# A re-ordered start, a shared last block and re-ordered routing steps in an attention kernel that feeds a mixture of experts

## The chip, the cores and the metric

The kernel runs on one core of one Trainium2 chip. The metric is the time of one execution on the device in microseconds (us); a run's profile gives in addition the span from the first to the last instruction of the core, which is 1 to 2 us shorter (261.74 and 260.6 in the profiled run before). Executions of one kernel are sorted into normal ("fast") and slow ones: of the kernel before, 257.84 to 261.46 us in five, and 262.16 and 262.80 in two. All comparisons here use fast runs, with a 95% interval.

The engines are named as in the profile: PE is TensorE (its weight loads are PEld), DVE is VectorE, ACT is ScalarE, POOL is GpSimd and SP is SyncE.

## The reference

Linear attention over 8 batches of 8 heads, 576 tokens and 64 numbers per head. Its output, 4608 tokens of 512 numbers, goes through the one best of 8 experts for each token.

```python
q_s = softmax(q, axis=-1);  k_s = softmax(k, axis=2)       # over numbers; over tokens
kv  = einsum('bhsd,bhse->bhde', k_s, v)
x   = einsum('bhsd,bhde->bhse', q_s, kv)                    # -> (4608, 512)

logits = x @ w_gate + modality_bias[modality_id]            # (4608, 8)
e_idx, gate_w = argmax(logits), softmax(logits) at e_idx
for e in range(8):
    mask = e_idx == e
    h = maximum(x[mask] @ w1[e], 0.0)                       # 512 -> 1024
    out[mask] = gate_w[mask, None] * (h @ w2[e])            # 1024 -> 512
```

The bias of a modality is large against the logits, so nearly every token goes to one of two experts, one for each modality. The kernel loads the weights of these two alone, computes all tokens with them, and checks by counts at the end whether that was everything (a loop behind it would do the rest; it runs zero times on these inputs).

## The kernel before

For each batch, `attend` makes kv, the logits and their inputs; `route` decides the side (expert) of each token and sorts. Sorting is a matmul with a permutation: side "a" is packed from the left of the array `xs`, side "b" from its right. `slots` and `places` find out which token sits at which place, for the stores. The feed-forward work on `xs` is a generator of *steps*: 8 first-layer matmuls (`h_ps`) or 4 second-layer ones (`y_ps`). `weave` lets a share of these steps run between the parts of a batch, so that PE has work while DVE and ACT go through the routing chain.

```python
CAP = 2432; NSLOT = 2 * CAP                     # places of a side: 19 blocks of 128
FULL = [256 * (b + 1) for b in range(B - 1)] + [CAP]
...
def route(b):
    ...                                         # logits -> kk (expert key) -> isa (side)
    yield 2
    r_ps = ...; matmul(r_ps[:, 0], tri, isa); matmul(r_ps[:, 1], ones, isa)     # places within the batch
    ...                                         # gsum, qi
    tensor_tensor_scan(out=aoff...); tensor_copy(out=aoff_i...)
    scale(0)                                    # x_sb of tile 0 <- x_ps * qi
    tensor_scalar(out=na, in0=isa...); tensor_tensor(out=pos, in0=na, in1=cpos...)
    tensor_tensor(out=pos, in0=pos, in1=r_ps[:, 0, :]...)
    tensor_tensor(out=perm...)
    yield 4
    for t in range(NT):                         # xT_ps = x_sb x perm; ACT copies it to xs at a run-time offset
        ...
def slots(b):                                   # DVE: vals, slot, hi, lo, hhi; POOL: hv = hhi * vals; DVE: hlo
def places(b):                                  # PE: id_ps = hlo x hv; DVE: lst, idb, ab, sel
    ...
    nc.vector.scalar_tensor_tensor(out=idb, in0=lst[:, 0, :], scalar=float(P), in1=lst[:, 1, :], ...)
    nc.vector.tensor_tensor(out=ab, in0=lst[:, 2, :], in1=krow, op=ALU.is_equal)
    nc.vector.scalar_tensor_tensor(out=sel, in0=idb, scalar=-OOB, in1=ab, ...)
...
def mains(n):
    for _ in range(n):
        if now[0] < 16 * len(sorted_) - 4: next(main, None); now[0] += 1
...                                             # the start, in part
alone(r0); slots(0); cast_weights(0, 3, nc.gpsimd); mains(1)
for _ in a1: mains(1)
places(0)
...
for b in range(2, B):
    weave(batch(b), 16 / 28.3, prep(b + 1, nc.gpsimd) if b + 1 < B else (), 4)
```

`prep(b, eng)` casts v of a batch on the named engine and takes the exponentials of k and q on ACT. `cast_weights(side, part, eng)` casts a quarter of an expert's weights to bf16.

The softmax here doesn't subtract the row's maximum and nothing guards it: scores larger than these inputs give would overflow.

Of the kernel before, what the change touches and what calls it, by code (L numbers as in the profile page):

```python
# [42 lines left out]
def kernel(  # L43
# [67 lines left out]
    def load_batch(b, names="kvq", eng=nc.sync):  # L111
        for nm in names:
            src = {"k": k, "v": v, "q": q}[nm]

            t = stage.tile([P, HG, NJ * Dh], FP32, name="st", tag="st")
            eng.dma_start(
                out=t,
                in_=bass.AP(
                    tensor=src.tensor,
                    offset=src.offset + b * H * S * Dh,  # L120
                    ap=[[NJ * Dh, P], [2 * S * Dh, HG], [1, NJ * Dh]],
                ),
            )
            st[nm, b] = t

    load_batch(0)
# [24 lines left out]
    load_batch(1)  # L151
# [67 lines left out]
    nc.gpsimd.memset(lst, 0.0)  # L219
    aoff_i = persist.tile([1, B * NT], I32)  # L220
# [8 lines left out]
    bsel = const.tile([P, B * NT, E], FP32)  # L229

# [42 lines left out]
    def gate_weights():  # L273
        nc.vector.tensor_copy(
            out=view(wgb, [[2 * Dh, E], [1, 2 * Dh]], 0, (0, NP)),
            in_=view(wg_f, [[1, E], [E, 2 * Dh]], 0, (0, NP)),
        )
        w_ps = sp_ps.tile([P, E, NP], BF16, name="w_ps", tag="sp")
        for e in range(E):
            nc.tensor.transpose(out=w_ps[:, e, :], in_=wgb[0:NP, 2 * Dh * e : 2 * Dh * (e + 1)], identity=ident[0:NP, 0:NP])  # L280
        nc.vector.tensor_copy(out=wg_sb, in_=view(w_ps, [[1, NP], [NP, E]]))

    def biases():

        nc.vector.tensor_copy(out=mbf, in_=view(mraw, [[2, NJ], [2 * NJ, 64]]))
        m_ps = sp_ps.tile([P, NT, B], BF16, name="m_ps", tag="sp")
        for t in range(NT):
            j0, nj = (2 * (t - 1), 2) if t else (NJ - 1, 1)
            nc.tensor.transpose(
                out=m_ps[0 : tsz[t], t, :], in_=view(mbf, [[1, 64 * nj]], 64 * j0), identity=ident[0:B, 0:B]  # L290
            )
        modf = const.tile([P, B, NT], FP32, name="modf")
        nc.vector.memset(modf, 0.0)
        nc.vector.tensor_copy(out=view(modf, [[1, NT - 1], [NT, B]], 1), in_=m_ps[:, 1:NT, :])
        nc.vector.tensor_copy(out=modf[0:64, :, 0], in_=m_ps[0:64, 0, :])
        biasd = const.tile([P, E], FP32, name="biasd")
        nc.vector.tensor_sub(out=biasd, in0=bias_b[:, 1, :], in1=bias_b[:, 0, :])
        nc.vector.tensor_tensor(
            out=bsel, in0=view(modf, [[1, B * NT], [0, E]]), in1=view(biasd, [[0, B * NT], [1, E]]), op=ALU.mult
        )  # L300
        nc.vector.tensor_tensor(
            out=bsel, in0=bsel, in1=view(bias_b, [[0, B * NT], [1, E]]), op=ALU.add
        )
# [42 lines left out]
    eks, eqs, last_v, xs_w = {}, {}, [None], []  # L346

    def prep(b, v_eng):
        eks[b] = sb.tile([P, NJ, HG * Dh], BF16, name="ek")
        eqs[b] = sb.tile([P, NJ, HG * Dh], BF16, name="eq")  # L350
        for nm in "kvq":
            src = st.pop((nm, b))
            for g in range(2):
                if nm == "v":
                    last_v[0] = copy_on(
                        v_eng,
                        view(vb_b[b % 2], [[Dh, 2], [260, NJ], [1, Dh]], 130 * g),
                        view(src, [[NJ * Dh, 2], [Dh, NJ], [1, Dh]], 2 * g * NJ * Dh),
                    )
                else:  # L360
                    nc.scalar.activation(  # L361
                        out=view((eks if nm == "k" else eqs)[b], [[Dh, 2], [HG * Dh, NJ], [1, Dh]], 2 * g * Dh),
                        in_=src[:, 2 * g : 2 * g + 2, :],
                        func=ACT.Exp,
                    )
                yield

    def attend(b):
# [38 lines left out]
        for c0, nj in ((0, 4), (4, 4), (8, 1)):  # L407
            tp = tps.tile([P, 1024], BF16, name="tp_ps", tag=tag)
            for jj in range(nj):
                for hp in range(2):  # L410
                    nc.tensor.transpose(  # L411
                        out=view(tp, [[2 * nj * 64, 2], [1, 64]], hp * nj * 64 + jj * 64),
                        in_=eq[:, c0 + jj, P * hp : P * hp + P],
                        identity=ident,
                    )
# [3 lines left out]
                view(tp, [[nj * 64, NP], [1, 64 * nj]]),  # L419
            )  # L420
            if nj > 1:
                yield 1.2 if c0 == 0 else 1.5
        kvT_ps = ka.tile([P, 1024], BF16, name="kvT_ps", tag="ka")
        for p_ in range(NP):
            nc.tensor.transpose(out=kvT_ps[:, P * p_ : P * p_ + P], in_=kvbd[:, p_, :], identity=ident)
        kvT = small.tile([P, NP * P], BF16, name="kvT")
        nc.scalar.copy(out=kvT, in_=kvT_ps[:, 0 : NP * P])
# [71 lines left out]
    def route(b):  # L499
# [19 lines left out]
        )  # L519
        xps = [x_tile(b, 0)]  # L520
        yield 1.6
        xps.append(x_tile(b, 1))
        yield 2
# [8 lines left out]

        nc.vector.tensor_tensor_scan(
            out=aoff[:, o + 1 : o + 1 + NT],
            data0=ones[:, 0:NT],
            data1=r_ps[:, 1, :],
            initial=aoff[:, o : o + 1],
            op0=ALU.mult,
            op1=ALU.add,
        )  # L540
        nc.vector.tensor_copy(out=aoff_i[:, o : o + NT], in_=aoff[0:1, o : o + NT])
# [12 lines left out]
        scale(0)  # L554
        na = small.tile([P, NT], FP32, name="na")
        nc.vector.tensor_scalar(out=na, in0=isa, scalar1=0.0, scalar2=None, op0=ALU.is_equal)
        pos = small.tile([P, NT], FP32, name="pos")
        nc.vector.tensor_tensor(out=pos, in0=na, in1=cpos, op=ALU.mult)
# [12 lines left out]
        yield 4  # L571
        scale(1)
        free[0] = nc.vector
        for t in range(NT):
# [13 lines left out]
            for side, off in (("a", 0), ("b", right)):  # L588
                a = nc.s_assert_within(at[t], 0, b * S + cum[t] - T, skip_runtime_bounds_check_because=WHY)
                w = nc.scalar.copy(out=window(a + off, b, T, off > 0), in_=xT_ps[:, :, 0:T])  # L590
                if b == 0 and t == 0:
                    after(w, xs_w, "every place holds a number, also one that no token comes to")
            yield 1.3 if t < NT - 1 else 2.5
# [59 lines left out]

    def todo_of(ph):
# [12 lines left out]
    def ffn1(lo, w, slot, hT):  # L667

        nf = 512 // w
        for f0 in range(0, KF, nf):  # L670
            h_ps = ff.tile([P, 512], FP32, name="h_ps", tag="ff")
            for f in range(nf):
                for kd in range(KD):
                    nc.tensor.matmul(  # L674
                        out=h_ps[:, f * w : (f + 1) * w],
                        lhsT=W[:, slot, kd * F + (f0 + f) * P : kd * F + (f0 + f + 1) * P],
                        rhs=xs[:, kd, lo : lo + w],
# [10 lines left out]
    def ffn2(w, slot, hT, ix, stores):  # L688
        for t in range(w // P):
            y_ps = ff.tile([P, D], FP32, name="y_ps", tag="ff")  # L690
            for kf in range(KF):
# [3 lines left out]
                    rhs=W[:, slot, W2 + kf * D : W2 + (kf + 1) * D],  # L695
# [3 lines left out]
                if kf == 3:  # L699
                    yield  # L700
            y_sb = ybuf.tile([P, D], FP32, name="y_sb")
# [16 lines left out]
    def second(lo, w, slot, hT):  # L718
        yield from ffn2(w, slot, hT, rows_of(sel, lo, w), "stores")

    def main_pieces():

        late = []
        for ph in range(NPH):
            for slot, lo, w in todo_of(ph):
                hT = hbuf.tile([P, KF, GW], BF16, name="hT")
                yield from ffn1(lo, w, slot, hT)
                late.append((lo, w, slot, hT))
                if len(late) > 1 or (ph, slot) == (0, 0):
                    yield from second(*late.pop(0))  # L730
        yield from second(*late.pop(0))

    main = main_pieces()
    now = [0]

    def mains(n):

        for _ in range(n):
            if now[0] < 16 * len(sorted_) - 4:
                next(main, None)  # L740
# [31 lines left out]
    for b in range(2, B):  # L772
        load_batch(b)
    gate_weights()
    biases()
    token_ids()
    p0, p1 = prep(0, nc.vector), prep(1, nc.gpsimd)
    a0, a1, r0, r1 = attend(0), attend(1), route(0), route(1)
    alone(p0)
    for kd in range(KD):  # L780
        for half in range(2):
            w = nc.gpsimd.memset(view(xs.bitcast(FP32), [[1, NSLOT // 4]], (2 * kd + half) * NSLOT // 4), 0.0)
            after(w, last_v, "GpSimd and VectorE share a port")
            xs_w.append(w)
    for _ in range(7):
        next(a0)
    next(p1)
    next(p1)
    alone(a0)
    next(r0)  # L790
    next(r0)
    next(r0)
    alone(p1)
    cast_weights(0, 0, nc.scalar)
    for _ in range(3):
        next(a1)

    next(r0)
    cast_weights(0, 2, nc.gpsimd)
    next(r0)  # L800
    next(a1)
    next(r0)
    next(a1)
    next(r0)
    next(a1)
    cast_weights(0, 1, nc.vector)
    alone(r0)
    slots(0)
    cast_weights(0, 3, nc.gpsimd)
    mains(1)  # L810
    for _ in a1:
        mains(1)
    places(0)
    cast_weights(1, 0, nc.scalar)
    next(r1)
    mains(1)
    cast_weights(1, 1, nc.scalar)
    next(r1)
    mains(1)
    next(r1)  # L820
    cast_weights(1, 2, nc.scalar)
    cast_weights(1, 3, nc.scalar)
    weave(r1, 0.6)
    slots(1)
    mains(8 - now[0])
# [17 lines left out]
    for b in range(2, B):  # L843
        weave(batch(b), 16 / 28.3, prep(b + 1, nc.gpsimd) if b + 1 < B else (), 4)
# [33 lines left out]
    for _ in main:  # L878
        pass
# [4 lines left out]
    with tc.For_i(0, nr) as e:  # L884
# [28 lines left out]
        for _, _, lo, w in passes:  # L913
            hT = hbuf.tile([P, KF, GW], BF16, name="hT")
            alone(ffn1(lo, w, 0, hT))
            alone(ffn2(w, 0, hT, rows_of(sel1, lo, w), "stores again"))
# [30 lines left out]
```

## Time and profile before

| | before |
|---|---|
| time, median of 3 runs | 261.74 us (258.37 to 262.39) |
| profiled span, mean granted PE clock | 260.6 us, 0.965 |
| PE / DVE / ACT / POOL busy | 202.9 / 148.8 / 144.5 / 81.4 us |
| first kv matmul of batches 2, 3, 7 | 67.66, 89.30, 184.82 us |
| end of the last matmul | 247.8 us |

A line of the timeline gives the start in us, the busy time of the group in us, the engine, the source line, the operation, output and inputs, shapes, the count and, in brackets, how long the engine had been idle before it and what ended that. Three timeline lines of the kernel before are needed later for comparison. The first two are the index arithmetic beside a cast of v on POOL; the third is the choice of side in batch 3, ahead of the sorting.

```profile
121.56 2.24 POOL L343 CAST vb<-st 128x1152 bf16<-128x1152 f32 x2
122.68 1.17 DVE L645 TENSOR_TENSOR ab<-lst,krow 128x38 f32<-128x38 f32 x1
...
128.72 0.23 DVE L517 SCALAR_TENSOR_TENSOR isa<-kk,key,valid 128x5 bf16<-128x5 f32 x1
```

`ab` takes 1.17 us beside POOL's second cast; it takes 0.19 at 47.90, with POOL idle. From `isa` at 128.72 to the first transposed tile at 132.02 (in the prediction) pass 3.30 us. The row of the page that gives PE's granted clock in tenths, in 40 slices of the span:

```profile
PEclk9999999979999869999999999999999999999985
```

The clock is full but for two short stretches, one before batch 2 (0.7 of full speed in the ninth slice, 52 to 59 us) and one at its end (0.8 and 0.6 in the 14th and 15th, 85 to 98 us); the last two slices (0.8 and 0.5) reach past PE's last matmul, which ends at 247.8 us.

### The profile page before, as it was taken

The numbers are of one execution on the slowest core, as the hardware profiler recorded it, in microseconds if no ns is written. First come the engines' busy times: TensorE is split into PE (matmuls) and PEld (weight loads), VectorE is DVE, ScalarE is ACT, GpSimd is POOL, SyncE is SP. The second block draws the span as 40 slices with busy tenths as digits, with TensorE's granted clock in tenths as the row PEclk, the third lists the DMA queues.
The fourth block names the chain that finished last, engine by engine and source line by source line (L and its number), as shares of the span: only waits on it lengthen the run. The fifth ranks groups of instructions, "written<-read, shape, count | busy, mean of one in ns | idle before, by whom it ended". The sixth has DMA issues, their size and how long they took to land. (4 is left out here: it accounts for less than half of the span.)

```text
span 260.6 us, 5319 instructions
## 1 busy us (share of the span) xinstructions
PE 202.9 (78%) x1994; PEld 140.6 (54%) x1994; DVE 148.8 (57%) x506; ACT 144.5 (55%) x230; POOL 81.4 (31%) x95
## 2 busy tenths in 40 slices
PE   0173659569997599898989889898987989999900
PEld 0062547347664475657557565755755656666500
DVE  5476773856628365768776786878658553111210
ACT  1344574797985646668576766756543734442200
POOL 5069205013360234126113611621232133222320
PEclk9999999979999869999999999999999999999985
DMA  6999999998799606932972020111202022221200
GB/s 226 373 391 406 390 400 344 314 381 333 242 378 397 237 3 219 309 139 57 376 227 95 3 81 29 54 43 40 84 3 81 1 83 81 81 83 72 82 16 1
DMA packets 18972, 46.58 MB, mean 179 GB/s; under 512 B 1261, under 2 KB 1261, under 8 KB 18942
## 3 DMA queue, kind: packets, MB, share of 16 engines
q1 hardware_dynamic: 15872, 36.70, 39.3%
q0 software_dynamic: 3040, 9.44, 9.5%
q8 instruction: 17, 0.28, 0.4%
q14 instruction: 13, 0.11, 0.1%
q10 hardware_dynamic: 30, 0.05, 0.1%
HBM read 36.75 MB, written 9.96 MB: 179 GB/s over the span
## 5 line engine op out<-in xcount | busy, mean ns | idle before, releaser
L674 PE MATMUL h_ps<-xs,W 128*128 128x256 bf16 (+1 forms) x640 | 78.9, 274 | 1.5 <-ACT xs L590 1.2
L703 POOL DMA_INDIRECT out_dram<-y_sb,ix x38 | 37.6, 988 | 124.1 <-DVE y_sb L343 48.7
L692 PE MATMUL y_ps<-W,hT 128*128 128x512 bf16 x304 | 74.3, 382 | 0.0
L674 PEld LDWEIGHTS <-W 128*128 128x128 bf16 x640 | 59.1, 100 | 11.3 <-issue 2.6
L685 ACT ACTIVATE hT<-h_ps 128x512 bf16<-128x512 f32 x69 | 40.6, 597 | 35.3 <-PE h_ps L674 32.8
L590 ACT CAST xs<-xT_ps 128x512 f32 (+2 forms) x80 | 38.1, 562 | 10.0 <-PE xT_ps L578 10.0
L692 PEld LDWEIGHTS <-hT 128*128 128x128 bf16 x304 | 27.4, 98 | 25.8 <-issue 0.6
L343 DVE COPY y_sb<-y_ps 128x512 f32<-128x512 f32 x19 | 13.1, 691 | 42.0 <-PE y_ps L692 41.0
L547 DVE TENSOR_TENSOR x_sb<-x_ps,qi 128x512 bf16<-128x512 f32 (+1 forms) x40 | 27.1, 682 | 0.9 <-PE x_ps L470 0.4
L578 PE MATMUL xT_ps<-perm,x_sb 128*128 128x128 bf16 (+1 forms) x160 | 16.0, 226 | 12.5 <-DVE perm L561 9.5
L343 ACT COPY y_sb<-y_ps 128x512 f32<-128x512 f32 x19 | 11.1, 582 | 22.9 <-PE y_ps L692 21.6
L578 PEld LDWEIGHTS <-x_sb 128*128 128x128 bf16 (+1 forms) x160 | 11.4, 103 | 21.0 <-issue 9.1
L361 ACT ACTIVATE eq<-st 128x1152 bf16<-128x1152 f32 x16 | 18.3, 1156 | 7.0 <-DMA st<-in_q_dram 4.7
L620 POOL TENSOR_TENSOR hv<-hhi,vals 128x570 bf16<-128x570 bf16 x8 | 12.5, 1568 | 28.1 <-DVE hhi L616 27.9
L361 ACT ACTIVATE ek<-st 128x1152 bf16<-128x1152 f32 x16 | 18.4, 1166 | 2.0 <-DMA st<-in_k_dram 2.0
L411 PE MATMUL tp_ps<-ident,eq 128*128 128x128 bf16 x144 | 14.1, 247 | 4.2 <-ACT et L343 2.0
L470 PE MATMUL x_ps<-kvbd,et 128*128 128x128 bf16 (+1 forms) x160 | 17.1, 235 | 0.0
L378 PE MATMUL kv_ps<-vb,ek 64*128 64x129 bf16 x288 | 12.8, 251 | 3.9 <-ACT eq L361 2.6
L343 POOL CAST vb<-st 128x1152 bf16<-128x1152 f32 x14 | 15.7, 1145 | 0.0
L411 PEld LDWEIGHTS <-eq 128*128 128x128 bf16 x144 | 11.7, 112 | 7.1 <-issue 3.6
L378 PEld LDWEIGHTS <-ek 64*128 64x128 bf16 x288 | 10.7, 111 | 6.4 <-ACT eq L361 2.7
L470 PEld LDWEIGHTS <-et 128*128 128x128 bf16 (+1 forms) x160 | 11.4, 107 | 4.5 <-issue 2.5
(139 smaller groups left out, 196.9 us busy)
## 6 DMA issues: line engine op xcount, KB each, us to landing
st<-in_k_dram SPq DMA_DIRECT2D x8, 1152.0 KB, 5.7
st<-in_v_dram SPq DMA_DIRECT2D x8, 1152.0 KB, 8.0
st<-in_q_dram SPq DMA_DIRECT2D x8, 1152.0 KB, 9.7
st<-in_moe_w_dram SPq DMA_DIRECT2D x8, 1024.0 KB, 8.7
out_dram<-y_sb,ix POOLq DMA_INDIRECT x38, 2.8
W<-in_moe_modality_id_dram ACTq DMA_DIRECT2D x1, 36.0 KB
hT<-in_moe_w_gate_dram ACTq DMA_DIRECT2D x2, 8.0 KB
bias<-n_moe_modality_bias_dram ACTq DMA_DIRECT2D x1, 0.1 KB
```

Source lines behind the costliest of these rows:

```text
L343: return (nc.scalar.copy if eng is nc.scalar else eng.tensor_copy)(out=out, in_=in_)
L361: nc.scalar.activation(out=view((eks if nm == "k" else eqs)[b], [[Dh, 2], [HG * Dh, NJ], [1, Dh]], 2 * g * Dh), in_=src[:, 2 * g : 2 * g + ...
L378: nc.tensor.matmul(out=kv[hg][:, 130 * hp : 130 * hp + 129], lhsT=ek[rows, j, P * hp : P * hp + P], rhs=vb[rows, j, hp, 0:129], start=(j = ...
L411: nc.tensor.transpose(out=view(tp, [[2 * nj * 64, 2], [1, 64]], hp * nj * 64 + jj * 64), in_=eq[:, c0 + jj, P * hp : P * hp + P], identity ...
L470: nc.tensor.matmul(out=view(x_ps, [[2 * Dh, 2], [1, Dh]], (4 * (p_ % 2) + p_ // 2) * Dh, (0, T)), lhsT=et[:, p_, tcol[t] : tcol[t] + T], r ...
L547: nc.vector.tensor_tensor(out=view(x_out[t], [[2 * Dh, HG], [Dh, 2], [1, Dh]], 0, (0, T)), in0=view(xps[t], [[2 * Dh, HG], [Dh, 2], [1, Dh ...
L578: nc.tensor.matmul(out=xT_ps[:, kd, 0:T], lhsT=x_out[t][0:T, kd * P : (kd + 1) * P], rhs=perm[0:T, t, 0:T], start=True, stop=True,)
L590: w = nc.scalar.copy(out=window(a + off, b, T, off > 0), in_=xT_ps[:, :, 0:T])
L674: nc.tensor.matmul(out=h_ps[:, f * w : (f + 1) * w], lhsT=W[:, slot, kd * F + (f0 + f) * P : kd * F + (f0 + f + 1) * P], rhs=xs[:, kd, lo ...
L685: nc.scalar.activation(out=h_out, in_=h_in, func=ACT.Relu)
L692: nc.tensor.matmul(out=y_ps, lhsT=hT[:, kf, t * P : (t + 1) * P], rhs=W[:, slot, W2 + kf * D : W2 + (kf + 1) * D], start=(kf == 0), stop=( ...
L703: store = nc.gpsimd.indirect_dma_start(out=out, out_offset=bass.IndirectOffsetOnAxis(ap=ix[:, t : t + 1], axis=0), in_=y_sb, in_offset=Non ...
```

## The change

The intent has four parts. One 128-place pass is dropped: the last block of both sides is replaced by one block, whose tokens and weights are copied at a run-time offset for whichever side is larger. The start is re-ordered so that batch 0 is sorted sooner, with v and q of batch 0 (and q of batch 1) loaded in halves. `xs` is cleared in parts, batch by batch. In the routing, the product for the permutation goes ahead of the counts and the scaling of tile 0 behind the permutation. The limit on feed-forward steps becomes a list of which batch each needs. The diff, cut to its core:

```diff
+    def clear(b):                                   # two memsets on GpSimd, left and right
+        lo, hi = S * b, min(S * (b + 1), NSLOT // 2)
+        xs_w[b] = [nc.gpsimd.memset(xs[:, :, c : c + hi - lo].bitcast(FP32), 0.0) for c in (lo, NSLOT - hi)]
+    clear(0)
+    clear(1)
 ...
 def route(b):
+        nc.vector.tensor_scalar(out=na, in0=isa, ...)         # before the counts
+        nc.vector.tensor_tensor(out=pos, in0=na, in1=cpos, ...)
-        yield 2
+        yield 2.4
 ...
-        scale(0)
-        ... na, pos
         ... perm
-        yield 4
+        scale(0)
+        yield 5
 ...
-            if now[0] < 16 * len(sorted_) - 4:
+            if now[0] < len(due) and due[now[0]] < len(sorted_):
 ...                                                 # order of passes from phase 2 on (1, 2: layer; x, y: passes)
+                order += [(ph, 1, x), (ph, 1, y), (ph, 2, x), (ph, 2, y)]
 ...                                                 # the start, from batch 0's sorting on
+    cast_weights(0, 1, nc.scalar)
+    alone(a1)
+    mains(1)
+    r1 = route(1)
+    cast_weights(0, 2, nc.scalar)
+    steps(r1, 1)
+    mains(1)
+    cast_weights(0, 3, nc.scalar)
+    steps(r1, 1)
+    mains(2)
+    steps(r1, 1)
     slots(0)
-    cast_weights(0, 3, nc.gpsimd)
-    mains(1)
-    for _ in a1:
-        mains(1)
+    cast_weights(1, 0, nc.gpsimd)
+    for b in range(2, 5):
+        clear(b)
+    mains(1)
     places(0)
-    cast_weights(1, 0, nc.scalar)
-    next(r1) ...
+    mains(1)
+    weave([next(r1)], 0.6)
+    cast_weights(1, 1, nc.vector)
+    weave(r1, 0.6)
     cast_weights(1, 2, nc.scalar)
     cast_weights(1, 3, nc.scalar)
-    weave(r1, 0.6)
+    mains(12 - now[0])
     slots(1)
 ...
-        weave(batch(b), 16 / 28.3, prep(b + 1, nc.gpsimd) ...)
+        weave(batch(b), (14 if b == 2 else 15.5) / 28.6, prep(b + 1, nc.gpsimd) ...)
 ...                                                 # the tail: which side is larger -> big_w, big_x
+    tail["x"] = ...; nc.vector.tensor_copy(out=tail["x"], in_=<xs at big_x>)
+    for i in range(2):
+        for half in range(2):
+            nc.vector.tensor_copy(out=t[:, ...], in_=<W at big_w + ...>)     # 4 copies of 128x2048 bf16
```

## The prediction

> **What bounds the kernel now.** I read the busy time by stretch first, then the instructions in order of time at each boundary that it shows, then the waits of TensorE (PE). The chain of waits is useless here: it holds two pieces in the last microsecond. The stretches (start:end, length, then busy us of PE, weight load, DVE, ACT, POOL, then the clock, the DMA share and GB/s):
>
> ```profile
> 0.00:37.90 37.90, 15.62 (x192) 13.26 (x193) 24.96 (x92) 17.21 (x22) 16.28 (x36) 1.00 0.98 364
> 37.90:67.60 29.70, 23.29 (x198) 16.66 (x195) 17.68 (x57) 22.46 (x32) 9.38 (x7) 0.94 0.90 319
> 67.60:90.20 22.60, 17.55 (x191) 11.27 (x190) 12.51 (x42) 16.88 (x27) 6.27 (x6) 0.97 0.95 357
> 90.20:115.20 25.00, 23.18 (x223) 16.14 (x223) 15.66 (x53) 15.28 (x27) 6.20 (x6) 0.89 0.48 164
> 212.70:247.80 35.10, 35.09 (x260) 22.39 (x258) 6.61 (x36) 13.08 (x22) 10.45 (x11) 1.00 0.20 74
> ```
>
> Time outside PE work is at the start. Until 37.9 us PE is idle 22.3 us; to 67.6 it is idle another 6.4; to 90.2 another 5.0. Then come batches of 23.07 us (the first kv matmuls of consecutive batches stand at 115.62, 138.69, 161.76 and 184.82), with about 21.3 us of PE work each. The last 35 us are feed-forward work alone, without a hole, so each matmul taken out there is time taken off the end. After PE's last matmul at 247.8 the kernel needs 12.8 us more to its end at 260.6, which the change leaves alone.
>
> Three places matter. First, the first feed-forward matmul:
>
> ```profile
> 13.90 1.42 DVE L343 CAST vb<-st 128x1152 bf16<-128x1152 f32 x2
> 14.80 2.13 PE L378 MATMUL kv_ps<-vb,ek 64*128 64x129 bf16 x36 [2.63 <-ACT eq L361]
> 23.82 2.24 POOL L343 CAST vb<-st 128x1152 bf16<-128x1152 f32 x2
> 23.87 1.15 DVE L505 TENSOR_TENSOR lg<-lg,bsel 128x40 f32<-128x40 f32 x1
> 31.07 1.88 ACT L343 CAST W<-st 128x2048 bf16<-128x2048 f32 x1
> 38.77 1.10 ACT L590 CAST xs<-xT_ps 128x512 f32 x2
> 39.43 1.86 PE L674 MATMUL h_ps<-xs,W 128*128 128x256 bf16 x8 [1.18 <-ACT xs L590]
> ```
>
> It starts at 39.43, released by the ACT copies of sorted tokens, not by the weights: the landing records put the second weight piece at about 27.2 us. The delay accumulates earlier. The v casts of batch 0 stand at 13.90 behind DVE work on gate weights and biases, though v landed at about 10.6; the routing's addition of 40 columns takes 1.15 us beside POOL's v cast; a weight cast of 1.88 us on ACT stands ahead of the copies of sorted tokens.
>
> Second, the end of batch 2:
>
> ```profile
> 88.32 0.38 PE L578 MATMUL xT_ps<-perm,x_sb 128*128 128x128 bf16 x4 [0.63 <-ACT xs L590]
> 89.30 0.29 PE L378 MATMUL kv_ps<-vb,ek 64*128 64x129 bf16 x1 [0.60 <-ACT xs L590]
> 90.27 2.11 PE L378 MATMUL kv_ps<-vb,ek 64*128 64x129 bf16 x35 [0.69 <-ACT xs L590]
> 115.62 1.20 PE L378 MATMUL kv_ps<-vb,ek 64*128 64x129 bf16 x36
> ```
>
> No feed-forward matmul stands between 84.3+1.03 and 92.31. The source says why: with two batches sorted the main work may go to 16x2-4 = 28 steps, and it has run out. PE then waits at every ACT copy, and 35 kv matmuls take 2.11 us where 36 take 1.20 a batch later: the slow clock.
>
> Third, one hole in each batch, and the last blocks:
>
> ```profile
> 132.02 0.27 PE L578 MATMUL xT_ps<-perm,x_sb 64*128 64x64 bf16 x4 [0.80 <-DVE perm L561]
> 237.15 1.95 PE L674 MATMUL h_ps<-xs,W 128*128 128x128 bf16 x32
> 238.93 3.62 PE L692 MATMUL y_ps<-W,hT 128*128 128x512 bf16 x16
> ```
>
> [...]the addition of 1.15 us took 0.20 at 49.00, with POOL idle.[...]
>
> **The change part by part.**
>
> (a) One block less. Both sides carry 19 blocks of 128 places, 38 in all; now the last block of each is dropped and one, chosen at run time, serves whichever side is larger. It saves one 128-wide pass: 32 first-layer matmuls, 1.95 us, and 8 second-layer ones, half of 3.62, 1.81 us. This lies in the full tail: **-3.8 us**. It adds four weight copies (4 x 0.69), a copy of tokens (some 0.4) and a register load on DVE (the like of it, 0.5 us): about 3.7 us. DVE is busy 6.6 of 35.1 us there, and the copies are issued some 25 us ahead of their use. A late output copy may hold a PSUM buffer: I allow +0.4.
>
> (b) The start. I carried the new order through, engine by engine, with durations from the trace. DVE can cast v at 9 to 11.3, so kv ends near 12.5 instead of 16.9. q in halves lets its first exponential go near 12.1, but the second half still lands at 13.6, so the exponentials end at 14.8 instead of 15.8. Logits come near 17.7 (before: 21.9). Routing takes about 3.4 us from there to the choice of side, near 21.2 (before: 26.95), now without POOL's v cast. Then gains shrink: ACT, not POOL, casts v of batch 1 (2.3), and q of batch 1 lands at 22.7, so ACT is held to 25.3. The 10 token copies (10 x 0.56 less the two short ones, 5.2 us) interleave with batch 1's copies (1.6), and DVE does batch 1's kv scaling and the token ids in between; they end near 35. The cast of the second weight piece (1.9) comes after them on ACT: first feed-forward matmul near 37 instead of 39.4. **-2.3 us**, and batch 1's attention is almost done by then (before, its logits came at 44.9).
>
> (c) No starvation. The new order lets 12 steps go with one batch sorted and 32 with two (before 28). 18 are meant to be done before batch 2 starts and 14 over it. So batch 3 starts with 32 steps done rather than 28, the 4 extra ones filling holes: 11.4 us of idle PE lie in 37.9 to 90.2. A step is 8 first-layer or 4 second-layer matmuls, 1.03 us at most and 0.9 pipelined: **-3.7 us**. The slow clock from 88.7 to 95.5 goes too: kv 0.9, two groups of 8 first-layer matmuls 0.85 and 0.4 (1.89 and 1.43 against 1.04), one of transposes 0.45: **-2.6 us**. Since ACT may not fill so neatly, I take 1.2 off these gains.
>
> (d) Batches 3 to 7. The product for the permutation is made before the counts are known, the scaling of the first tile goes behind the permutation, and the wait weighs 5 instead of 4, so 0.45 step more work is in between. The first transposed matmul then needs the scaled tile as well, so of the 0.8 hole I count 0.5 gone: 5 x 0.5 = **-2.5 us**. Main work per batch falls from 16 to 15.5 steps, but what is not done there goes to the tail, no gain.
>
> (e) Memsets of sorted x: eight of 1.11 us at 15.4 to 23.9 become smaller ones, the first four at 5 to 9 us on an idle POOL. No own gain.
>
> Sum: -3.8 +0.4 -2.3 -3.7 -2.6 +1.2 -2.5 = -13.3, from 261.7 to **248.4 us**.
>
> **Rivals.** ACT becomes the bound of the start: it is busy 22.5 of 29.7 us in 37.9 to 67.6 already and gets v of batch 1 and two weight casts beside the relus. For it: each relu there stands behind a 1.9 us cast, and PE waits for it. Against: POOL and DVE keep three casts, as before. Then (b) and half of (c) go: about 253. Second, loading is the bound: it moves 364 GB/s to 37.9 us, so halves of a transfer bring no byte earlier. Against: weights land 12 us before use. Were it so, only (a) and (d) stay: 255 to 256. Third, the end: weight copies that wait (register load, a buffer, an in-order DVE with output copies behind) would stall the tail by some us, giving back (a): 252. Fourth, the batch becomes bound by its own latency once it carries less main work; for it speaks the 1.75 us idle per batch, against it that holes follow single waits; it would cancel (d): 251.
>
> **Range and chances.** Each rival alone leaves a gain of over 2% (below 256.5); two at once are needed to lose it. The three runs before spread from 258.4 to 262.4, so I give 242.5 to 254.5. Faster by over 2%: 0.92, within: 0.07, slower: 0.01.
>
> **What will show it.** (a) 37 stores instead of 38, 608 first-layer matmuls instead of 640 and 296 instead of 304 second-layer ones, and a tail without a hole ahead of the last pass. (b) First h_ps matmul near 37, r_ps of batch 0 near 21.5. (c) No stretch at half clock after 60 us, and feed-forward matmuls between all transposed tiles of batch 2. (d) The hole before the first transposed matmul under 0.4 us, its releaser x_sb, batches of about 22.1 us. I would be wrong if the first h_ps came after 39, if holes moved to another wait (relu behind casts), or if a batch took 23 us with 15.5 steps.

## The result, and the profile after

The changed kernel takes **267.37 us** (median of 4 runs, 267.25 to 268.03) against 260.88 us (258.37 to 262.39) for the kernel before: ratio **1.029** (1.020 to 1.037). It is slower, where the prediction said 5% faster. A ratio here is the mean time of one kernel's fast runs over that of the other's in the same rounds, so it is not quite the ratio of the medians quoted. The profiled spans are 260.6 us before and 265.6 after; the mean clock of these two runs is 0.965 and 0.910.

First, where the span went. Starts of the first kv matmul of a batch cut it into stretches; all numbers are us, read from PE's timeline.

| stretch | before | after | after less before |
|---|---|---|---|
| start to batch 2 | 67.66 | 75.61 | +7.95 |
| batch 2 | 21.64 | 20.49 | -1.15 |
| batch 3 | 26.32 | 23.78 | -2.54 |
| batches 4 to 6 | 69.20 | 71.09 | +1.89 |
| batch 7 to the last matmul | 63.0 | 61.5 | -1.5 |
| after the last matmul | 12.8 | 13.1 | +0.3 |
| span | 260.6 | 265.6 | +5.0 |

The loss is before batch 2. The first two stretches also hold more work than before: by the counts of weight loads, 18 feed-forward steps stand before batch 2 and 13 over it, against 16 and 12. And starts differ between runs: batch 2 starts at 67.66 us in the kernel before and at 64.81 in the experiment with the tail alone (below), whose code is the same up to there. So some 3 us of a difference in this start can be chance; the loss is larger than that.

In the clock row of the changed kernel half clock and mixtures with it (0.5 to 0.9 of full speed; 0.65 on average from 20 to 73 us) reach from the fourth slice to the eleventh, some 20 to 73 us. This is not what makes it slow: other runs of the same kernel with a mean clock of 0.942 and 0.944 took 268.03 and 267.40 us.

```profile
PEclk9995557759799999999999999999999999999975
```

The start itself goes as planned. These are the counts of batch 0 and the first first-layer matmuls behind the weight cast, from the timeline of the changed kernel:

```profile
22.00 0.17 PE L568 MATMUL r_ps<-isa,tri 128*128 128x5 bf16 x1 [2.98 <-DVE isa L556]
...
38.12 1.46 PE L726 MATMUL h_ps<-xs,W 128*128 128x256 bf16 x6 [1.70 <-ACT W L358]
```

`r_ps` stands at 22.00 (27.09 before). Two first-layer matmuls go at 35.84 and the others wait for the second weight piece until 38.12 (39.43 before). The loss comes after that. The timeline of the changed kernel from 49 to 75 us:

```profile
49.80 0.52 PE L676 MATMUL id_ps<-hv,hlo 64*128 64x114 bf16 x5 [4.10 <-POOL hv L659]
...
51.52 4.56 POOL L228 MEMSET xs<- 128x1152 f32 x6
...
52.01 4.09 DVE L690 TENSOR_SCALAR ix<-sel 128x2 int32<-128x2 f32 x1
...
52.09 4.02 DVE L580 TENSOR_TENSOR x_sb<-x_ps,qi 128x512 bf16<-128x512 f32 x1
...
56.19 0.61 PE L617 MATMUL xT_ps<-perm,x_sb 128*128 128x128 bf16 x4 [3.52 <-DVE x_sb L580]
...
63.03 3.71 ACT L358 CAST W<-st 128x2048 bf16<-128x2048 f32 x2
...
67.29 6.19 PE L726 MATMUL h_ps<-xs,W 128*128 128x256 bf16 x40 [2.69 <-ACT hT L737]
...
74.87 0.17 DVE L690 TENSOR_SCALAR ix<-sel 128x2 int32<-128x2 f32 x1
```

There are three holes on PE, 10.3 us together:

1. **4.10 us** for `id_ps`. `slots(0)` now stands directly ahead of `places(0)`, and in DVE's list, which the trace shows worked off in order, it stands behind batch 1's permutation (45.38) and first scaling (46.12): its first instruction starts at 46.73. POOL's product `hv` ends only at 49.75, and on PE nothing behind `id_ps` starts in that time. Before, feed-forward steps and batch 1's attention lay between the two.
2. **3.52 us** for a transposed tile. Six memsets of `xs`, a row of 4.56 us on POOL, hold a DVE instruction of two numbers per partition (`ix`) for 4.09 us; the same instruction takes 0.17 at 74.87. The held one ends at 56.10, the row of memsets at 56.08. The scaling of the next tile (`x_sb`) is queued behind it: it is recorded from 52.09 and ends at 56.11. Not every instruction is held: at the start of the same trace, in the row of the first four memsets (4.88 to 9.02 us), casts of 16 and of 2 numbers (`parts`) take 1.26 and 0.90 us (0.15 for 16 numbers at 4.31, ahead of the row), and a subtraction of two SBUF inputs between them, at 5.99, takes 0.16.
3. **2.69 us** for first-layer matmuls: the relu that frees their buffer waits behind two weight casts, 3.71 us, on ACT.

Second, the batches. The timeline of the changed kernel around the index arithmetic in batch 4:

```profile
128.08 2.56 DVE L681 SCALAR_TENSOR_TENSOR idb<-lst 128x38 f32<-128x38 f32 x1
...
128.35 2.24 POOL L358 CAST vb<-st 128x1152 bf16<-128x1152 f32 x2
...
131.35 0.67 PE L479 MATMUL lg_ps<-gx,et 128*128 128x18 bf16 x20 [0.89 <-DVE gx L474]
```

Here an instruction of two SBUF inputs (`idb`) is held over both casts of v, 2.56 us, where before `ab` was held over one, 1.17 us; the logits behind it now wait 0.89 us. (`ab` is recorded from 122.68, 1.12 us into two casts of 2.24. `idb` is recorded from 128.08 and the casts from 128.35, so which of them came first the trace does not settle.) This stands in batches 3 and 4 alone; in batches 5 and 6 `idb` takes 0.20 us. And a batch carries less main work than the prediction's 15.5 steps: between 120.6 and 145.0 us 64 weight loads of the first layer stand as before, but 28 of the second layer instead of 32, that is 8 + 7 = 15 steps instead of 16. (`weave` starts its account at zero in each batch, so 15.5 is cut to 15. Of the 14 meant for batch 2, 13 are done.) The window's answer for the second layer, with start:end, length, and busy us of PE and of the weight loads:

```profile
120.60:145.00 24.40, 6.54 (x25) 2.48 (x28) 1.00 0.54 187
```

(25 matmuls are recorded for 28 loads: some matmul records are missing, so the loads are counted.)

The tail goes as planned. Timeline of the changed kernel:

```profile
224.97 2.50 DVE L996 COPY st<-W 128x2048 bf16 x4
...
245.35 1.95 PE L726 MATMUL h_ps<-x_sb,st 128*128 128x128 bf16 x32
...
250.59 1.89 PE L744 MATMUL y_ps<-st,hT 128*128 128x512 bf16 x8
```

The weight copies are done 18 us ahead of their use (227.5 and 245.35 us), 37 stores, 608 first-layer matmuls and 296 weight loads of the second layer are recorded, and no hole stands before the last pass.

### The profile page after: what moved, and what is told of

The parts are those of the page before. It is cut to its first block, busy times and chain, and to the rows that moved or that the text cites.

```text
span 265.6 us, 5231 instructions
## 1 busy us (share of the span) xinstructions
PE 200.6 (76%) x1934; PEld 137.4 (52%) x1954; DVE 151.4 (57%) x501; ACT 153.8 (58%) x241; POOL 78.7 (30%) x94
## 5 line engine op out<-in xcount | busy, mean ns | idle before, releaser
L726 PE MATMUL h_ps<-xs,W 128*128 128x256 bf16 x576 | 74.2, 282 | 4.7 <-ACT hT L737 2.7
L744 PE MATMUL y_ps<-W,hT 128*128 128x512 bf16 x268 | 68.9, 386 | 1.3 <-issue 0.3
L757 POOL DMA_INDIRECT out_dram<-y_sb,ix x37 | 36.7, 991 | 111.9 <-DVE y_sb L358 29.9
L726 PEld LDWEIGHTS <-W 128*128 128x128 bf16 x576 | 55.7, 101 | 14.3 <-issue 3.6
L737 ACT ACTIVATE hT<-h_ps 128x512 bf16<-128x512 f32 x73 | 42.0, 596 | 21.1 <-PE h_ps L726 20.3
L629 ACT CAST xs<-xT_ps 128x512 f32 (+2 forms) x80 | 38.8, 563 | 13.6 <-PE xT_ps L617 13.3
L358 ACT COPY y_sb<-y_ps 128x512 f32<-128x512 f32 x22 | 12.9, 586 | 43.2 <-PE y_ps L744 40.9
L580 DVE TENSOR_TENSOR x_sb<-x_ps,qi 128x512 bf16<-128x512 f32 (+1 forms) x40 | 29.8, 764 | 1.2 <-PE x_ps L509 0.5
L358 DVE COPY y_sb<-y_ps 128x512 f32<-128x512 f32 x15 | 10.4, 692 | 33.0 <-PE y_ps L744 33.0
L393 PE MATMUL kv_ps<-vb,ek 64*128 64x129 bf16 x288 | 12.8, 239 | 5.9 <-DVE vb L358 2.8
L393 PEld LDWEIGHTS <-ek 64*128 64x128 bf16 x288 | 10.3, 104 | 9.7 <-issue 7.6
L358 POOL CAST vb<-st 128x1152 bf16<-128x1152 f32 x12 | 13.5, 1152 | 0.0
```

The source lines that it names most:

```text
L358: return (nc.scalar.copy if eng is nc.scalar else eng.tensor_copy)(out=out, in_=in_)
L393: nc.tensor.matmul(out=kv[hg][:, 130 * hp : 130 * hp + 129], lhsT=ek[rows, j, P * hp : P * hp + P], rhs=vb[rows, j, hp, 0:129], start=(j = ...
L580: nc.vector.tensor_tensor(out=view(x_out[t], [[2 * Dh, HG], [Dh, 2], [1, Dh]], 0, (0, T)), in0=view(xps[t], [[2 * Dh, HG], [Dh, 2], [1, Dh ...
L629: w = nc.scalar.copy(out=window(a + off, b, T, off > 0), in_=xT_ps[:, :, 0:T])
L726: nc.tensor.matmul(out=h_ps[:, f * w : (f + 1) * w], lhsT=w1(kd * F + (f0 + f) * P, P), rhs=x_in[:, kd, :], start=(kd == 0), stop=(kd == K ...
L737: nc.scalar.activation(out=h_out, in_=h_in, func=ACT.Relu)
```

## The experiments

Sixteen kernels ran, in four calls; all gave the correct result. The kernels of a call share the runs of the kernel before on the same chip; its medians, over all its runs, slow ones among them, were 259.85, 261.92, 261.48 and 259.23 us in that order.

### First call: each hole by itself

**Clears earlier.** If the row of memsets makes hole 2, moving it away should give that hole back.

```diff
     cast_weights(0, 0, nc.gpsimd)
+    for b in range(2, 5):
+        clear(b)
 ...
     cast_weights(1, 0, nc.gpsimd)
-    for b in range(2, 5):
-        clear(b)
```

> Only the last three clearings of sorted x (six GpSimd memsets) move, from the routing of batch 1 to the time right after GpSimd's first weight cast (near 27 us). Theory: these memsets hold VectorE out for 4 us (the index computation took 4.09 us beside them, the same one 0.17 later), so TensorE's hole of 3.5 us at 52.7 to 56.2 goes, and with it some of the half clock: 3 to 5 us faster than the changed kernel (267.4), near 263. Rival: the hole has another cause (the register loads of the offsets, a PSUM buffer): then it stays and the time stays at 267.

Measured: 266.25 us, ratio 1.025 (1.016 to 1.035), so no gain that the interval carries. Hole 2 is gone, but the first six matmuls behind the weight cast moved from 38.12 to 43.10. The memsets now stand at 27.58, and two of DVE's token ids are recorded there with 5.53 and 4.60 us (0.59 and 0.17 in the changed kernel), with batch 0's scaling behind them. The place was badly chosen: the hold had moved, not gone.

**Slots earlier.** `slots(0)` goes ahead of batch 1's second routing step, so `hv` is made while DVE is idle.

```diff
     steps(r1, 1)
+    slots(0)
     mains(1)
     cast_weights(0, 3, nc.scalar)
 ...
     steps(r1, 1)
-    slots(0)
     cast_weights(1, 0, nc.gpsimd)
```

> Only the place computation of batch 0 moves ahead of the routing counts of batch 1, into VectorE's idle time of 2.4 us at 39.7 to 42.2. Theory: the hole of 4.1 us ahead of the place matmuls (waiting for GpSimd's product at 48.1 to 49.8) goes; since the next hole (the memsets) stays and moves forward, 2 to 5 us faster than 267.4. Rival: the permutation of batch 1, later on the same in-order engine, is put off by as much, and the time stays within 1 us.

Measured: 260.42 us, ratio 1.002 (0.991 to 1.013). Batch 2 starts at 71.05 instead of 75.61. PE still waits 4.20 us before `id_ps`, but now for DVE: the memsets have moved forward with POOL's work to 44.59 and hold a DVE cast of five numbers (`aoff_i`) for 4.30 us (0.16 at 23.27 in the changed kernel). One wait had hidden the other; of two holes one is left.

**Casts earlier.** The last two weight casts on ACT go ahead of batch 1's transposed tiles.

```diff
     mains(1)
+    cast_weights(1, 2, nc.scalar)
+    cast_weights(1, 3, nc.scalar)
     weave([next(r1)], 0.6)
     cast_weights(1, 1, nc.vector)
     weave(r1, 0.6)
-    cast_weights(1, 2, nc.scalar)
-    cast_weights(1, 3, nc.scalar)
```

> Only the two last weight casts on ScalarE move, from after the routing of batch 1 to ahead of its first tile, where the kernel before has them and where ScalarE idles 3.9 us (52.9 to 56.9). Theory: the hole of 2.7 us at 64.6 to 67.3, where matmuls wait for relus standing behind 3.7 us of casts, goes: 2.5 to 4 us faster than 267.4, with the clock staying full from 60 us on. Rival: the casts now delay the copies of sorted tokens by as much; same time.

Measured: 263.24 us, ratio 1.016 (1.006 to 1.025). The 2.69 us hole is gone and batch 2 starts at 69.87. The casts here (from 52.02) fall into the time in which the memsets (50.78, 4.56 us) hold DVE anyway: `ix` takes 4.10 us from 51.26.

**All three.**

> All three moves together. Theory: the holes of 4.1, 3.5 and 2.7 us (10.3) go and most of the half clock between 50 and 71 us (some 3 us), so batch 2 starts near 64 instead of 75.6 and the time is 254 to 257. Rival: the routing of batch 1 is bound by its own chain of VectorE and ScalarE, and only one hole's worth (3 to 5 us) is won: 262 or more.

Measured: 260.92 us, ratio 1.009 (0.997 to 1.020), no better than the slots alone. The timeline shows why:

```profile
42.66 1.46 PE L726 MATMUL h_ps<-xs,W 128*128 128x256 bf16 x6 [1.90 <-ACT W L358]
...
51.41 3.70 ACT L358 CAST W<-st 128x2048 bf16<-128x2048 f32 x2
...
55.72 0.53 PE L617 MATMUL xT_ps<-perm,x_sb 128*128 128x128 bf16 x4 [2.60 <-ACT xs L629]
```

The clears at their early place cost the start 4.5 us, and the casts, with no memset hold to hide in, now delay the copies of the sorted tokens by 2.60 us. The causes are right; two of the three cures were not.

### Second call: cures that hit nothing else, and the tail by itself

**Clears alone, in the gap of DVE.** The row of memsets is released by DVE's last cast of v of batch 0, about 11.4 us, where DVE waits for data: in the changed kernel it is idle 0.62 us before 12.32 and 0.82 before 13.40, and its inputs from 11.51 to 15.1 us are matmul results (`w_ps`, `m_ps`, `kv_ps`) and numbers made from them.

```diff
-    def clear(b):
+    def clear(b, behind=()):
 ...
+        for w in xs_w[b] if behind else ():
+            after(w, behind, 'VectorE casts v first')
 ...
     steps(p0, 4)
+    for b in range(2, 5):
+        clear(b, last_v)
 ...
-    for b in range(2, 5):
-        clear(b)
     mains(1)
     places(0)
```

> Changed kernel with only the last clearings moved, released after VectorE's last v cast of batch 0 (11.4 us). Theory[...]: the 4.1 us index computation near 52 falls to 0.2 and the hole of 3.5 us goes, with the first feed-forward matmul still near 38: 262 to 264.5. Rival: same time as changed (267), the hole comes back as another wait.

Measured: 262.09 us, ratio 1.008 (0.998 to 1.018). Batch 2 starts at 70.66, 4.95 us earlier than in the changed kernel. From its timeline:

```profile
38.53 1.46 PE L728 MATMUL h_ps<-xs,W 128*128 128x256 bf16 x6 [1.69 <-ACT W L360]
...
49.48 0.74 PE L678 MATMUL id_ps<-hv,hlo 64*128 64x114 bf16 x5 [4.10 <-POOL hv L661]
...
62.34 6.19 PE L728 MATMUL h_ps<-xs,W 128*128 128x256 bf16 x40 [2.69 <-ACT hT L739]
```

Holes 1 and 3 stand unchanged at 4.10 and 2.69 us, hole 2 is gone (`ix` takes 0.17 us), and the first matmul is where it was. The same memsets, moved to where DVE has none of the instructions that they held elsewhere, give back 4.95 us, and the logits of batch 0 end at 18.36, as in the changed kernel (18.35): the hold is shown.

**All three cures.** Clears as above, slots early, and the last two weight casts on DVE behind `slots(1)`.

```diff
     steps(r1, 1)
+    slots(0)
 ...
-    slots(0)
     cast_weights(1, 0, nc.gpsimd)
-    ... clears
 ...
-    cast_weights(1, 2, nc.scalar)
-    cast_weights(1, 3, nc.scalar)
     mains(12 - now[0])
     slots(1)
+    cast_weights(1, 2, nc.vector)
+    cast_weights(1, 3, nc.vector)
```

> Changed kernel with the place computation of batch 0 early (as e2_slots), the last clearings released right after VectorE's last v cast of batch 0 (near 11.4 us, where VectorE then works from PSUM), and the last two weight casts on VectorE after the places of batch 1 instead of on ScalarE. Theory: clearing at 27 us in e4_all3 only moved the lock (first feed-forward matmul at 42.7 instead of 38.1), and the casts ahead of the tiles held the token copies (2.6 us); with both away batch 2 starts near 64.5 instead of 69.3, time 255 to 257. Rival: the clearing between 11 and 16 us holds VectorE as well; then the first logits come 3 us or more later and the time stays near 260.

Measured: **255.16 us, ratio 0.976** (0.968 to 0.985): from 2.9% slower to 2.4% faster (the interval lies below 1, but does not exclude a gain of less than 2%). Its timeline:

```profile
48.81 0.40 PE L619 MATMUL xT_ps<-perm,x_sb 128*128 128x128 bf16 x4 [0.83 <-DVE x_sb L582]
...
64.13 1.20 PE L395 MATMUL kv_ps<-vb,ek 64*128 64x129 bf16 x36
```

Of the 3.52 us 0.83 is left, and batch 2 starts at 64.13, 11.5 us earlier than in the changed kernel (75.61). The batches 3 to 6 are as long as in the changed kernel, within 0.06 us each.

**The tail alone.** The kernel before with the shared last block and nothing else (the copies of the diff above, with `rows_of_last` and the register load, which it leaves out).

> The kernel before with one part of the change alone: the last block of either side dropped and one block of places served by run-time offset, with its copies of weights and tokens on VectorE. Theory: one 128-wide pass less in a full tail, 3.8 us less minus at most 0.4: 256.0 to 256.6 where before has 259.9, ratio 0.986 to 0.988. Rival: the copies (3.7 us of VectorE) or the register load stall the tail and give it back: ratio 0.995 to 1.0.

Measured: 256.07 us, ratio 0.985 (0.975 to 0.995), about 4 us less than before. In its trace 59.9 us lie between the start of batch 7 and the end of the last matmul, against 63.0: 3.1 less, near the predicted 3.4. (The rest of the difference of the two traces lies before batch 2, at 64.81 instead of 67.66, where the code is the same.) Part (a) of the prediction holds by itself.

**The old spacing and rate.** The changed kernel with the waits 1.5, 2, 4, 1.3 and 2.5 and 16 steps per batch, as before.

```diff
-                    yield 1.2 if c0 == 0 else 2
+                    yield 1.2 if c0 == 0 else 1.5
-        yield 2.4
+        yield 2
-        yield 5
+        yield 4
-            yield 1.2 if t < NT - 1 else 1.3
+            yield 1.3 if t < NT - 1 else 2.5
-        weave(batch(b), (14 if b == 2 else 15.5) / 28.6, ...)
+        weave(batch(b), (14 if b == 2 else 16) / 28.3, ...)
```

> Changed kernel with the old spacing in the batches: weights 1.5, 2, 4, 1.3 and 2.5 and rate 16/28.3 (14/28.3 for batch 2), all else as changed. Theory: the new spacing does 15 steps per batch (0.5 of 15.5 is lost where each batch starts its count at 0) in 23.55 us where the old did 16 in 23.07; undoing it wins 0.5 per batch and 5 steps of the tail: 5 to 7 us, near 261, with first matmuls of consecutive batches 23.1 apart. Rival: the slow batches come from the new order of passes (two first layers, then two second layers); then batches stay at 23.5 or more and only the steps are regained: 264 or more.

Measured: 267.55 us, ratio 1.027 (1.019 to 1.035), the same as the change. Batches are 25.13 us with 16 steps. The theory that the new spacing makes the batches long fell.

### Third call: what makes the batches long

The theory left: the new order of passes (1x, 1y, 2x, 2y), the new rate, or both. All four kernels start from the three cures (255.16 us).

```diff
-                order += [(ph, 1, x), (ph, 1, y), (ph, 2, x), (ph, 2, y)]
+                order += [(ph, 1, x), (ph, 2, x), (ph, 1, y), (ph, 2, y)]
```

> e7_fix with one edit: from the third phase on, the passes go first layer, second layer, first layer, second layer, as near to the old order as the gate of sorted batches allows, instead of two first and two second layers. Theory: the new order of passes, not the spacing, makes the batches long (e5_yields took 25.1 us for 16 steps with the old spacing, before took 23.07): batches fall from 23.5 to about 22.5, four to five batches, 3 to 5 us: 250 to 252. Rival: the routing's own re-ordering makes them long; then no change (255).

The order alone: 253.95 us, ratio 0.979 (0.968 to 0.990).

> e11_order with the old spacing and rate too (16 steps per batch). Theory: batches of 23.1 us as in the kernel before, with 5 steps less in the tail than e7_fix: 249 to 252. Rival: batches stay near 25, as in e5_yields: 254 to 256.

Order, old spacing and old rate together: 254.27 us, ratio 0.984 (0.972 to 0.995).

> e7_fix with one number changed: the rate of batches 3 to 7 from 15.5 to 16.01, so that 16 steps and not 15 fall in each batch. Theory of the lost half step: the batch has holes that the 16th step fills in part, so a batch grows by less than a step's 0.95 us, and the tail loses 5 steps: 1 to 4 us faster than e7_fix. Rival: the batch grows by a full step or more (as e5_yields, 25.1): same or slower.

The rate alone, 16.01 for 15.5 so that a batch does get 16 steps: 253.24 us, ratio 0.977 (0.969 to 0.987).

> e11_order with the rate 16.01. Theory: order and rate together give batches with every hole filled, 23 us each with 16 steps: 248 to 251, the fastest of the four. Rival: as fast as e11_order within 1 us, since steps only move between batch and tail.

Order and rate: 253.69 us (5 runs, 251.12 to 253.87), ratio 0.979 (0.969 to 0.988).

The four medians lie within 1.1 us of each other, and the ratios (0.977 to 0.984) stand beside 0.976 for the three cures alone, with intervals that overlap. The expectations for the order, for all three and for order and rate (248 to 252 us) failed; that for the rate (1 to 4 us less than 255.16) fits. So neither the order of passes nor the rate alone is what the missing microseconds hang on. With 16 steps a batch takes 24.23 us (rate alone, batches 4 to 6), 24.74 (order, spacing, rate) and 24.24 (order, rate), against 23.07 before. The timeline of order, spacing and rate together, batch 4, shows what they share:

```profile
114.92 2.56 DVE L683 SCALAR_TENSOR_TENSOR idb<-lst 128x38 f32<-128x38 f32 x1
...
118.18 0.67 PE L481 MATMUL lg_ps<-gx,et 128*128 128x18 bf16 x20 [0.83 <-DVE gx L476]
...
122.12 0.23 DVE L558 SCALAR_TENSOR_TENSOR isa<-kk,key,valid 128x5 bf16<-128x5 f32 x1
...
125.42 0.29 PE L619 MATMUL xT_ps<-perm,x_sb 64*128 64x64 bf16 x4 [1.05 <-DVE x_sb L582]
```

The hold of 2.56 us is there again; in the kernels with 16 steps it stands in each of the batches 3 to 6. And from `isa` to the first transposed tile pass 125.42 - 122.12 = 3.30 us, exactly as before the change (and in the changed kernel itself, 114.55 - 111.25 in batch 3): the re-ordered routing saves nothing, since DVE goes through the same list of instructions without a pause (no idle time is recorded before any of them in those 3.30 us).

### Fourth call: VectorE's hold beside the casts of v

The casts of v on POOL are made to wait for the end of the index arithmetic (`sel`); nothing else changes.

```diff
-                    last_v[0] = copy_on(
+                    last_v[0] = v_cast = copy_on(
                         v_eng, ...
                     )
+                    if v_eng is nc.gpsimd and b > 2:
+                        after(v_cast, sel_w, 'the index arithmetic goes first')
 ...
-        nc.vector.scalar_tensor_tensor(out=sel, ...)
+        sel_w[:] = [nc.vector.scalar_tensor_tensor(out=sel, ...)]
```

On order, spacing and rate:

> e12_order_spacing with GpSimd's v casts waiting for the end of the index operations of the batch before. Theory (GpSimd's two v casts hold the two-input index operation for 2.2 us, and the chain from it to the logits and the routing sets the batch): that operation falls from 2.5 to 0.2 us, batches from 24.7 to about 23.2, five times 1.5: 247 to 249 against 254.3. Rival: the length comes from the new position of the tile scaling behind the permutation; then the operation is short but batches stay near 24.5 and the time near 254.

Measured: 252.38 us, ratio 0.972 (0.966 to 0.978). Batches 24.11 instead of 24.74, and not the expected 23.2: the instruction is short (0.28 us on average over the kernel, 1.46 without the wait), and the batches stay nearly as long as the expectation's rival said.

On order and rate:

> e14_order_rate16 with the same wait. Theory: batches from 24.24 to about 22.8, 5 to 7 us: 247 to 249, the fastest kernel. Rival: as e14 (253.7), since v of the next batch comes 2 us later and its kv matmuls wait for it.

Measured: **248.66 us (247.37 to 249.03), ratio 0.958** (0.954 to 0.962): the fastest kernel of all, 4.2% faster than the kernel before. Batches 23.18 instead of 24.24. Its timeline, at the same place:

```profile
115.47 0.20 DVE L686 SCALAR_TENSOR_TENSOR idb<-lst 128x38 f32<-128x38 f32 x1
...
116.09 2.24 POOL L360 CAST vb<-st 128x1152 bf16<-128x1152 f32 x2 [0.35 <-DVE sel L690]
...
117.67 0.66 PE L483 MATMUL lg_ps<-gx,et 128*128 128x18 bf16 x20
```

`idb` takes 0.20 us, the casts start after `sel`, and the logits wait for nothing. From the start of batch 3 to that of batch 7 pass 177.74 - 84.36 = 93.38 us, against 179.79 - 82.17 = 97.62 without the added wait: 4.2 us less.

On the kernel before:

> The kernel before with the same wait. Theory: its operation of 1.17 us falls to 0.2 and each of five batches wins at most 1 us: ratio 0.983 to 0.995. Rival: that hold lay beside other waits (the logits did not wait for it there): ratio 1.0.

Measured: 259.66 us, ratio 0.999 (0.990 to 1.008): no gain. (Its profiled run was a slow one, so its trace is not used.) The hold of 1.17 us before the change cost nothing that the time shows.

On the changed kernel, with nothing else:

> The changed kernel with the same wait and nothing else. Theory: only its odd batches (24.75 and 24.3) are held, by 1.5 each; the others (22.03, 23.78) are not: batches near 22.5 throughout, 3 to 5 us faster than 267.4: 262.5 to 264.5. Rival: no change.

Measured: 265.73 us, ratio 1.024 (1.019 to 1.028). Batches 3 to 6 take 92.83 us instead of 94.87: 2.0 us, the share of this hold in the changed kernel itself. Which batches were held, the expectation had wrong, and the time fell less than it said. The two that were held, 3 and 4, are 0.97 and 1.07 us shorter (22.81 and 23.68); 5 and 6, which were not, moved by 0.02 each (22.05 and 24.29). In batch 3:

```profile
104.80 0.20 DVE L684 SCALAR_TENSOR_TENSOR idb<-lst 128x38 f32<-128x38 f32 x1
```

## Why the prediction was wrong

**(a) One block less: right.** Predicted -3.8 + 0.4, and the tail alone gave a ratio of 0.985, about 4 us. In the trace of the changed kernel the weight copies take 0.69 us each and the copy of tokens 0.29, and no hole precedes the last pass. The third rival (the end stalls) is out.

**(b) The start: right as far as it went.** The logits of batch 0 were predicted near 17.7 (an end, as the 21.9 before) and ended at 18.35; `r_ps` was predicted at 21.5 and came at 22.00; the first matmul, predicted near 37, came at 35.84 for two and 38.12 for the rest.

**(e) "No own gain": the step that failed first.** The text took the memsets to be harmless and looked at the first four of them only. The other six stand in the middle of the sorting of batch 1 and hold a DVE instruction for 4.09 us. Moving them alone brought batch 2 forward by 4.95 us. No rival mentioned them, though the prediction itself sets the addition of 1.15 us beside POOL's v cast against 0.20 us with POOL idle.

**(c) "the 4 extra ones filling holes": the step that failed with it.** The engines' order was carried through to about 37 us and no further; from there the prediction counted idle PE time of the kernel before and assumed that it would be filled. In the changed order three new holes of 10.3 us stand between 45 and 68 us. From (b) batch 2 should have started at 67.66 - 2.3 = 65.4; it started at 75.61, and with the three causes taken away at 64.13. So the expectation of 65.4 was near, and the loss is these three: `hv` (not seen), the memsets (dismissed), and the relu behind casts. The last is the first rival ("each relu there stands behind a 1.9 us cast"), which was given too little weight and put at the wrong place. What (c) promised for batch 2 did come: 20.49 us instead of 21.64, no starvation, and batch 3 without its slow clock, 23.78 instead of 26.32. But batch 3 starts with 31 steps done and not 32, since batch 2 got 13 of its 14. As to that clock: the pair 2.11 / 1.20 does show a slow one (granted 0.50 from 90 to 94 us), and in the changed kernel 1.00 is granted from 75.61 to 119.90. That filled holes would keep it full was the estimate: between 82 and 90 us PE was busy 4.3 us, and its longest pause was 1.14 us. What exactly slowed the clock there no run shows.

**(d) "5 x 0.5 = -2.5": wrong in sign.** The sign that the text named did come. Before the first transposed tile PE is idle 0.21 us in batch 3 and shows no idle time in batches 4 to 6, instead of 0.80, and the releaser is `x_sb`:

```profile
114.55 0.29 PE L617 MATMUL xT_ps<-perm,x_sb 64*128 64x64 bf16 x4 [0.21 <-DVE x_sb L580]
```

The failed step is that the lost idle time was booked as lost batch time. The hole was read as a wait for `perm` that re-ordering could shorten, but the chain behind it is DVE's own unbroken work: 3.30 us before and after, so the tile comes no earlier. Instead of 22.1 us the batches 3 to 6 took 94.87 / 4 = 23.7, with 15 steps and not 15.5. In place of the saving came a longer hold at `idb`, whose removal is worth 2.0 us in the changed kernel, where two batches have it, and 4.2 in order and rate, where four have it. At its best, 23.18 us with 16 steps, the new batch equals the old one (23.07).

**The sum.** Predicted -13.3, measured +5.0 in span: 18.3 apart. Batch 2 is 10.2 later than (b) says; batches 3 to 6 are 94.87 - 4 x 22.1 = 6.5 longer; the remaining 1.6 are not divided further. The steps cut to whole numbers (31 for 32, 15 for 15.5 in each batch) were left for the tail and belong to it.

**The chances** rested on "two at once are needed to lose it". Two did come at once (relus behind casts, and batches that stayed long), and two things that were in no rival. The chance of 0.01 for slower was far too small for a change that re-orders the engines' lists over 40 us that were not carried through.

**Open.** With the hold removed and nothing else (the last experiment) batches 3 to 6 of the changed kernel still take 23.2 us on average with 15 steps, so of the 6.5 us the hold explains 2.0 and the rest has no shown cause. With the old order, spacing and rate and the hold removed a batch still takes 24.11 us instead of 23.07; waits of 1.05 and 0.70 us for the scaled tile and of 0.69 for `hv` are in its trace. Whether that comes from the order in the routing or from the phase of passes against batches was not separated. Why order and rate gain 1.06 us per batch from the wait for `sel`, and order, spacing and rate only 0.63, was not settled either.

## What to carry to other kernels

When work is re-ordered over engines that work off their lists in order (here `x_sb` and a weight cast, next in DVE's list, ended at 56.11 and 57.17, behind `ix` at 56.10), carry every engine's list through to the point where the old and new order meet again; idle time of the old order is not a place that new work will fill. A memset or cast on GpSimd that looks idle-time work can hold one tiny VectorE instruction (here `ix`, 4.09 us instead of 0.17, beside memsets, and `idb`, 2.56 instead of 0.20, beside casts), and with it everything behind: place such rows where VectorE has none of the instructions that the traces show held, and check the move with a run, since a hold easily moves along instead of going away (here to 5.53 us on a token id, and to 4.30 on `aoff_i`). A wait before an instruction is worth removing only if what releases it can come earlier; the chain of back-to-back instructions on DVE here, 3.30 us, was not shortened by changing their order.
